# Attention's TensorE work of a batch in six stretches, not seven: windowed attention and a snake MLP in one kernel

## The chip, the cores and the metric

The kernel runs on one core of a Trainium2 chip. The metric is device microseconds (us) of one execution. The core's engines each work through their own list of instructions in order: PE (TensorE: matmuls, with its weight loads shown apart as PEld), ACT (ScalarE), DVE (VectorE), POOL (GpSimd) and SP (SyncE, which issues DMAs). They wait for each other by semaphores alone.

## What is computed

Eight batches of eight heads, 576 tokens of width 64: attention in a band of 32 tokens to each side, plus eight global tokens that see and are seen by all; then, on all 4608 tokens, two matmuls with the snake function between them.

```python
scores = q @ k.T / sqrt(64)                    # per batch and head, 576 x 576
mask = |i - j| <= 32  or  i is global  or  j is global
attn = softmax(where(mask, scores, -1e9))
x = (attn @ v) as 4608 x 512
h = x @ w_in                                   # 512 -> 2048
g = h + sin(alpha * h)**2 / alpha
out = g @ w_out                                # 2048 -> 512
```

## The kernel before

The work alternates between two kinds of phase. `gemm1(b)` multiplies batch b's attention output `xT` by `w_in`, in 16 groups of 8 matmuls (line 1113); ACT takes the sine of a group (line 1160), DVE or ACT squares it, and DVE adds the linear part (line 1166, `H<-s,recipT,z`), which is the last reading of the group's PSUM bank. Group nt writes the banks `zn`, `zr`, `zd` in turn, so that the last, nt = 15, stands in `zn`, and nt = 14 in `zd`.

Then `phase_a(b + 1, b)` does the attention of batch b+1, and beside it runs `gemm2(b)`, the product with `w_out` (line 1218, banks `zo`), as filler: it is a generator, and each `fill(n)` in the attention's code issues its next n matmuls (128x512). When 16 of them have ended, ACT copies the block out (line 1225) and SP stores it.

Attention goes over four pairs of heads, hp 0 to 3. For one pair there are two units of scores, `scores(hp, 0)` and `scores(hp, 1)`, each of 14 small 64x64 matmuls (line 814), an exponential on ACT that reads their bank (line 822), and a multiplication with the mask on DVE (`cover`, line 831). `denominators(hp)` are 28 small matmuls of E with ones into `zd` (line 862), a logarithm on ACT (line 772), and a small sum of the same bank on DVE, `GD` (line 756). `inverse(hp)` is an exponential of that logarithm on ACT, `R` (line 779). `numerators(hp)` are 28 small matmuls of E with the values into `zn` (line 862 too), the product with R on DVE (`normalise`, line 908, `xT<-zn,R`), and a small sum `GN`. A unit that writes a bank waits until the last reader of the bank's earlier content is done. Scores go to the bank `zs` (the profile's `ring`) but for two of the eight units.

In short letters, s for scores, d for denominators, n for numerators, and the filler matmuls in parentheses, PE's list in one attention phase is: (7), s00 s01 (10), s10 s11 d0 (8), s20 n0 (5), s21 d1 (5), s30 n1 (5), s31 d2 (7), n2 d3 n3 (3). A run of units between two fillers is called a stretch here. There are seven stretches, and 50 filler matmuls around them (in the first such phase the 10 and the 8 are 9 and 9). `beside(hp)` adds DVE work of other kinds after some stretches: squares of the batch before (lines 1027 to 1031), and the placing of the next batch's queries (line 366). `place_globals` is a copy on ACT (lines 374, 377).

Batch 0 has an order of its own (`first_batch`), so the order described runs seven times, for batches 1 to 7. Pools: `pairp` holds E, four buffers; `logp` holds the logarithms, five.

Of the kernel before, what the change touches and what calls it, by code (L numbers as in the profile page):

```python
# [12 lines left out]
DT = mybir.dt  # L13
# [3 lines left out]
P = 128  # L17
# [3 lines left out]
WCOL = 120  # L21
# [228 lines left out]
def kernel(  # L250
# [11 lines left out]
    nc = tc.nc  # L262
    B, H, S, D = q.shape
# [4 lines left out]
    NT6 = NT12 // 2  # L268
    NK = KT + NG
    NHP = H // 2  # L270
# [20 lines left out]
    pairp = mctx.enter_context(tc.tile_pool(name="pairp", bufs=4))  # L291
# [79 lines left out]
    def place_globals(b, part, copy):  # L371

        if part == 0:
            copy(out=KX[b % 2][:, :, :, KT:NK], in_=kTg[:, :, None, :, b].to_broadcast([P, NHP, NT12, NG]))
        else:
            y = part - 1
            copy(
                out=globals_of(b, slice(0, P), y),
                in_=qTg[:, :, None, y::2, b].to_broadcast([P, NHP, 7, 4]),
            )  # L380

    def globals_of(b, rows, y):

        q0 = QX[b % 2][rows, :, y, PAD : PAD + 4]
        return bass.AP(
            tensor=q0.tensor, offset=q0.offset, ap=[list(q0.ap[0]), [2 * QROW, NHP], [SEG, 7], [1, 4]]
        )
# [74 lines left out]
    zn, zd = [banks.tile([P, 2, 512], DT.float32, name=name) for name in ("zn", "zd")]  # L462
# [286 lines left out]
    def begin(i):  # L749

        m = i // 2
        return SEG * m - PAD if i % 2 == 0 else SEG * m + 12

    def global_sums(b, hp, key, z):
        g0 = z[:, 0, 0, 0:4]
        nc.vector.tensor_reduce(
            out=(GN, GD)[key][:, hp, :, b].rearrange("p (c x) -> p x c", x=2),
            in_=bass.AP(
                tensor=g0.tensor, offset=g0.offset,
                ap=[list(g0.ap[0]), [256, 2], [1, 4], [512, 2], [SEG, 4]],  # L760
            ),
            axis=AX.XY, op=ALU.add,
        )

    def tokens(z):
        return z.rearrange("p k x c -> p (k x) c")[:, :, 0 : 3 * SEG].rearrange(
            "p k (m c) -> p k m c", c=SEG
        )[:, :, :, 4:]

    def logarithm(b, hp, den):  # L770
        L = logp.tile([P, 4, 3, KT], DT.float32, name="L")
        nc.scalar.activation(out=L[:], in_=den, func=AF.Ln, scale=2.0**-SHIFT)  # L772
        r0 = b * H + 2 * hp
        nc.sync.dma_start(out=LC[r0 : r0 + 2, :], in_=L[0:P:D].rearrange("p k m c -> p (k m c)"))
        return L

    def inverted(L):
        R = normp.tile([P, 4, 3, KT], DT.float32, name="R")
        nc.scalar.activation(out=R[:], in_=L[:], func=AF.Exp, scale=-1.0, bias=shift[:, 0:1])
        return R  # L780

    def attention(b, beside):
# [7 lines left out]
        Es, Ls, Rs, begun = {}, {}, {}, set()  # L790
        ring = tc.alloc_tile_pool(name="ringp", bufs=1, space=PSUM)
        zs = ring.tile([P, 2, 512], DT.float32, name="ring")
# [3 lines left out]
        def windows(half):  # L796


            last = half * (NT6 - 1)
            return [(half * NT6 + m, m, 16 * (m == 0 == half), 60 - 16 * (m == half * last > 0)) for m in range(NT6)] + [  # L800
                (NT6 - half, last, 44 * half, 16 + 44 * half)
            ]

        def scores(hp, g):
            z = {(0, 1): zd, (1, 1): zn}.get((hp, g), zs) if b else (zs, zn)[g]
            for e in range(NT6 + 1):
                for half in range(2):
                    i, m, c0, c1 = windows(half)[e]
                    if m // G3 != g:
                        continue  # L810
                    s0 = PAD + begin(i)
                    for t in range(2):
                        rows = slice(t * D, (t + 1) * D)
                        nc.tensor.matmul(  # L814
                            out=z[half * D : (half + 1) * D, t, 0 : G3 * WCOL].rearrange(
                                "p (m x c) -> p m x c", x=2, c=60
                            )[:, m % G3, :, c0:c1],
                            lhsT=kx[rows, hp, i, :],
                            rhs=qx[rows, hp, :, s0 + c0 : s0 + c1],
                            start=True, stop=True, skip_group_check=True,  # L820
                        )
            nc.scalar.activation(out=weights(hp, g), in_=z[:, :, 0 : G3 * WCOL], func=AF.Exp, scale=scale)  # L822
            if b:
                cover(hp, g)

        def weights(hp, g):
            return Es[hp][:, :, G3 * g : G3 * (g + 1), :].rearrange("p t m c -> p t (m c)")

        def cover(hp, g):
            Eg = weights(hp, g)  # L830
            nc.vector.tensor_tensor(  # L831
                out=Eg, in0=Eg,
                in1=MASKT[:, None, G3 * g : G3 * (g + 1), :].rearrange("p o m c -> p o (m c)").to_broadcast(
                    [P, 2, G3 * WCOL]
                ),
                op=ALU.mult,
            )

        def nd(hp, key):


            if b == 0:
                t = zd if key or hp == last else (pair["zr"], zn)[hp % 2]
            else:
                t = (zn, zd)[key] if hp < last else (pair["zr"] if key else zd)
            return t[:].rearrange("p k (x c) -> p k x c", x=2)

        def products(hp, key):


            for e in range(NT6 + 1):
                for half in range(2):
                    i, m, c0, c1 = windows(half)[e]
                    s0 = begin(i)
                    lo, hi = (0, CUT + 4) if half == 0 else (CUT, QLEN)
                    if e == NT6:
                        lo, hi = (lo, CUT) if half == 0 else (CUT + 4, hi)
                    a, z = max(s0 + c0, lo), min(s0 + c1, hi)
                    rows = slice(half * D, half * D + NK)
                    for t in range(2):  # L860
                        bank = (hp, key, half, t)
                        nc.tensor.matmul(  # L862
                            out=nd(hp, key)[t * D : (t + 1) * D, half, :, a - half * CUT : z - half * CUT],
                            lhsT=ones[rows, 0:D] if key else values(b, rows, half, i, 2 * hp + t),
                            rhs=Es[hp][rows, t, m, :].rearrange("p (x c) -> p x c", x=2)[:, :, a - s0 : z - s0],
                            start=bank not in begun, stop=True, skip_group_check=True,
                        )
                        begun.add(bank)
# [21 lines left out]
        def denominators(hp):  # L890
            products(hp, 1)
            Ls[hp] = logarithm(b, hp, tokens(nd(hp, 1)))
            global_sums(b, hp, 1, nd(hp, 1))

        def inverse(hp):
            Rs[hp] = inverted(Ls[hp])
# [6 lines left out]
        def numerators(hp):  # L903
            products(hp, 0)
            normalise(hp)

        def normalise(hp):
            nc.vector.tensor_tensor(
                out=xT[:, hp, 0:S].rearrange("p (k m c) -> p k m c", k=4, c=KT), in0=tokens(nd(hp, 0)),
                in1=Rs[hp][:], op=ALU.mult,  # L910
            )
            global_sums(b, hp, 0, nd(hp, 0))
# [49 lines left out]
        last = NHP - 1  # L962
# [2 lines left out]
            return  # L965
        fill(START)
        beside(-1)
        for hp in range(NHP):
            newest[0] = Es[hp] = pairp.tile([P, 2, NT6, WCOL], DT.bfloat16, name="E")
            scores(hp, 0)  # L970
            if hp > 1:
                inverse(hp - 2)
                numerators(hp - 2)
                fill(FIRST[hp])
            scores(hp, 1)
            if hp and 0 < b and b + 1 < B:
                place_globals(b + 1, hp - 1, nc.scalar.copy)
            if hp:
                denominators(hp - 1)
            fill((SECOND_FIRST if b == 1 else SECOND)[hp])  # L980
            beside(hp)
        release_ring()
        inverse(last - 1)
        numerators(last - 1)
        denominators(last)
        products(last, 0)
        inverse(last)
# [288 lines left out]
    waiting, copied, at_group, newest = [], [None], [None], [None]  # L1276

    def fill(n):
        while n and waiting:
            if next(waiting[0], None) is None:  # L1280
                waiting.pop(0)
            else:
                n -= 1

    START = 7
    FIRST, SECOND, SECOND_FIRST = (0, 0, 5, 5), (10, 8, 5, 7), (9, 9, 5, 7)
    AFTER_COPY = 2

    NEAR = 3
# [70 lines left out]
    E = mybir.EngineType  # L1360
# [34 lines left out]
```

## Time and profile before

| | |
|---|---|
| time, median of 3 runs | 340.67 us (340.37 to 340.89) |
| the profiled execution's own time | 340.73 us |
| span of its profile | 339.0 us |
| busy: PE, ACT, DVE, POOL | 310.8, 278.5, 253.9, 142.5 us |
| filler matmuls `zo` (line 1218) | 134.3 us busy |
| granted TensorE clock | 9 tenths or more in all 40 slices |

A busy PE is not PE at its peak: the ends of matmuls are modelled, and the small matmuls of attention overlap each other. The chain of waits tells how much time each piece adds to the path: its rows give the start, the time to the next piece of the path, and the piece. An attention phase spans about 15 us on PE, one of `gemm1` about 20 us.

### The profile page before, as it was taken

How to read it: one execution, taken by the hardware profiler on the slowest of the kernel's cores; microseconds unless marked ns; L12 is line 12 of the kernel's file. 1: busy time of each engine (PE TensorE's matmuls, PEld its weight loads, DVE VectorE, ACT ScalarE, POOL GpSimd, SP SyncE). 2: the span in 40 equal slices, each digit the busy share in tenths (PEclk: the TensorE clock that was granted, in tenths of full speed). 3: DMA queues.
4: the chain of work that ended last, by engine and by line, in shares of the span. 5: the costliest groups of instructions: out<-in, count | busy, mean ns of one | idle time of the engine just before them, and what ended most of it. 6: DMA issues, size and time to landing. Idle time of an engine off the chain costs nothing.

```text
span 339.0 us, 11821 instructions
## 1 busy us (share of the span) xinstructions
PE 310.8 (92%) x4753; PEld 202.9 (60%) x4812; DVE 253.9 (75%) x485; ACT 278.5 (82%) x405; POOL 142.5 (42%) x296
## 2 busy tenths in 40 slices
PE   0778999999999999999999999999999999999994
PEld 0665765567556765667556755676566755665543
DVE  4784896877885888687886788578858788778930
ACT  6784888988999889988898889888888888889621
POOL 7983323339615761656345652458060000003600
PEclk9999999999999999999999999999999999999999
DMA  7999999989999999999959993799999311010232
GB/s 105 114 167 205 187 223 162 169 135 129 191 144 112 197 121 131 105 122 186 151 87 138 170 168 81 78 116 201 164 115 140 68 33 69 1 33 0 80 93 68
DMA packets 141941, 42.00 MB, mean 124 GB/s; under 512 B 126426, under 2 KB 136794, under 8 KB 141882
## 3 DMA queue, kind: packets, MB, share of 16 engines
q0 software_dynamic: 100096, 18.51, 69.6%
q1 hardware_dynamic: 41786, 22.69, 34.9%
q8 instruction: 38, 0.62, 0.8%
q14 instruction: 21, 0.17, 0.2%
HBM read 41.95 MB, written 20.77 MB: 185 GB/s over the span
## 4 chain that ended last, share of the span: by engine, by line
PE 77%; DVE 7%; ACT 6%; issue 4%; DMA 3%; POOL 2%; DVEq 0%; POOLq 0%; ACTq 0%
PE zo L1218 32%; PE zn L1113 13%; PE zr L1113 10%; PE zd L1113 9%; PE ring L814 4%; DVE H L1166 3%; PE zd L862 3%; ACT sb L1160 2%; PE zn L862 2%; DVE s L1165 1%; DMA H<-in_q_dram 1%; DMA out_dram<-osb 1%; ACT L988 1%; ACT s L1163 1%; ACT L L772 1%
## 5 line engine op out<-in xcount | busy, mean ns | idle before, releaser
L1218 PE MATMUL zo<-w_out,H 128*128 128x512 bf16 (+1 forms) x517 | 134.3, 377 | 6.1 <-issue 5.1
L1113 PEld LDWEIGHTS <-w_in 128*128 128x128 bf16 x1024 | 100.3, 98 | 46.0 <-issue 10.0
L1218 PEld LDWEIGHTS <-H 128*128 128x128 bf16 x592 | 53.6, 98 | 46.2 <-issue 0.4
L1113 PE MATMUL zn<-xT,w_in 128*128 128x288 bf16 (+1 forms) x384 | 58.0, 291 | 3.5 <-DVE H L1166 2.8
L1113 PE MATMUL zr<-xT,w_in 128*128 128x288 bf16 x320 | 48.5, 291 | 0.3
L1160 ACT ACTIVATE sb<-zn,alphaT 128x576 bf16<-128x576 f32 (+1 forms) x48 | 35.6, 742 | 14.7 <-PE zn L1113 14.2
L1166 DVE SCALAR_TENSOR_TENSOR H<-s,recipT,zn 128x576 bf16<-128x576 bf16 (+1 forms) x48 | 39.5, 822 | 10.4 <-ACT s L1163 6.5
L1113 PE MATMUL zd<-xT,w_in 128*128 128x288 bf16 x320 | 46.3, 288 | 0.4 <-DVE H L1166 0.2
L1165 DVE TENSOR_TENSOR s<-sb 128x576 bf16<-128x576 bf16 (+1 forms) x70 | 32.6, 465 | 14.4 <-ACT sb L1160 14.2
L822 ACT ACTIVATE E<-ring 128x720 bf16<-128x720 f32 x46 | 35.9, 780 | 8.7 <-PE ring L814 8.2
L1163 ACT ACTIVATE s<-sb 128x576 bf16<-128x576 bf16 (+1 forms) x58 | 40.0, 689 | 1.8
L831 DVE TENSOR_TENSOR E<-E,MASKT 128x720 bf16<-128x720 bf16 x64 | 33.4, 529 | 8.0 <-ACT E L822 6.1
L1166 DVE SCALAR_TENSOR_TENSOR H<-s,recipT,zd 128x576 bf16<-128x576 bf16 (+1 forms) x40 | 32.9, 822 | 7.6 <-ACT s L1163 5.0
L1166 DVE SCALAR_TENSOR_TENSOR H<-s,recipT,zr 128x576 bf16<-128x576 bf16 (+1 forms) x40 | 32.9, 822 | 6.5 <-ACT s L1163 4.9
L344 POOL DMA_DIRECT2D kd<-in_k_dram x48 | 31.2, 653 | 9.1 <-issue 7.3
L1160 ACT ACTIVATE sb<-zd,alphaT 128x576 bf16<-128x576 f32 (+1 forms) x40 | 29.6, 739 | 5.2 <-PE zd L1113 5.1
L1160 ACT ACTIVATE sb<-zr,alphaT 128x576 bf16<-128x576 f32 (+1 forms) x40 | 29.6, 740 | 4.3 <-PE zr L1113 4.3
L1208 POOL COPY H<-H 128x11 bf16 (+1 forms) x16 | 7.2, 452 | 57.6 <-DVE H L1166 56.7
L346 POOL DMA_DIRECT2D vd<-in_v_dram x48 | 30.4, 643 | 1.8 <-issue 1.3
L1225 ACT COPY osb<-zo 128x512 f32<-128x512 f32 (+1 forms) x36 | 21.0, 582 | 10.7 <-PE zo L1218 7.0
L346 POOL DMA_DIRECT2D qd<-in_q_dram x40 | 25.3, 633 | 8.2 <-issue 5.1
L814 PEld LDWEIGHTS <-KX 64*64 64x64 bf16 x896 | 15.5, 113 | 19.7 <-issue 18.8
(170 smaller groups left out, 375.3 us busy)
## 6 DMA issues: line engine op xcount, KB each, us to landing
VF<-vd SPq DMA_DIRECT2D x14, 336.0 KB
kd<-in_k_dram POOLq DMA_DIRECT2D x48, 72.0 KB, 4.6
vd<-in_v_dram POOLq DMA_DIRECT2D x48, 72.0 KB, 3.8
qd<-in_q_dram POOLq DMA_DIRECT2D x40, 72.0 KB, 6.3
w_out<-in_moe_w_out_dram POOLq DMA_DIRECT2D x2, 1024.0 KB, 26.0
out_dram<-osb SPq DMA_DIRECT2D x7, 256.0 KB
out_dram<-osb SPq DMA_DIRECT2D x8, 224.0 KB
out_dram<-osb SPq DMA_DIRECT2D x8, 192.0 KB
```

The lines of the kernel that those rows point to most:

```text
L344: nc.gpsimd.dma_start(out=dst[:, :, h], in_=src.rearrange("(i a) d -> a i d", a=KT))
L346: nc.gpsimd.dma_start(out=dst[:, h], in_=src)
L814: nc.tensor.matmul(out=z[half * D : (half + 1) * D, t, 0 : G3 * WCOL].rearrange("p (m x c) -> p m x c", x=2, c=60)[:, m % G3, :, c0:c1], l ...
L822: nc.scalar.activation(out=weights(hp, g), in_=z[:, :, 0 : G3 * WCOL], func=AF.Exp, scale=scale)
L831: nc.vector.tensor_tensor(out=Eg, in0=Eg, in1=MASKT[:, None, G3 * g : G3 * (g + 1), :].rearrange("p o m c -> p o (m c)").to_broadcast([P, ...
L1113: nc.tensor.matmul(out=h_part, lhsT=w_in[:, c, nt * P : (nt + 1) * P], rhs=xT[:, c, lo:hi], start=(c == 0), stop=(c == CT - 1), skip_group ...
L1160: nc.scalar.activation(out=sb[:, 0:W], in_=h, func=AF.Sin, scale=alphaT[:, nt : nt + 1])
L1163: nc.scalar.activation(out=s2[:, 0:W], in_=sb[:, 0:W], func=AF.Square)
L1165: nc.vector.tensor_tensor(out=s2[:, 0:W], in0=sb[:, 0:W], in1=sb[:, 0:W], op=ALU.mult)
L1166: nc.vector.scalar_tensor_tensor(out=H2[:, nt, r0 : r0 + W], in0=s2[:, 0:W], scalar=recipT[:, nt : nt + 1], in1=h, op0=ALU.mult, op1=ALU.add,)
L1218: nc.tensor.matmul(out=ops[:, cols], lhsT=H2[:, nt, blk * P : (blk + 1) * P], rhs=w_out[:, nt, cols], start=(nt == 0), stop=(nt == NT - 1) ...
L1225: nc.scalar.copy(out=osb[:, cols], in_=ops[:, cols])
```

## The change

The loop over pairs becomes a table `STEPS` that says which units a stretch holds and how many filler matmuls follow it. In the short letters the new list is: (7), s00 s01 s10 (13), s11 d0 s20 (8), s21 d1 n0 (7), s30 d2 n1 (7), s31 n2 (5), d3 n3 (3). These are six stretches; the units and the 50 filler matmuls are the same. The two units whose bank changes are s10, which moves from `zs` to `zn`, and s20, which moves from `zs` to `zn`; s11 moves from `zn` to `zs`. `inverse(step - 2)` stands at the start of a step, and `place_globals` at its end, behind the units.

```diff
         def scores(hp, g):
-            z = {(0, 1): zd, (1, 1): zn}.get((hp, g), zs) if b else (zs, zn)[g]
+            z = {(0, 1): zd, (1, 0): zn, (2, 0): zn}.get((hp, g), zs) if b else (zs, zn)[g]
...
-        for hp in range(NHP):
-            newest[0] = Es[hp] = pairp.tile([P, 2, NT6, WCOL], DT.bfloat16, name="E")
-            scores(hp, 0)
-            if hp > 1:
-                inverse(hp - 2)
-                numerators(hp - 2)
-                fill(FIRST[hp])
-            scores(hp, 1)
-            if hp and 0 < b and b + 1 < B:
-                place_globals(b + 1, hp - 1, nc.scalar.copy)
-            if hp:
-                denominators(hp - 1)
-            fill((SECOND_FIRST if b == 1 else SECOND)[hp])
-            beside(hp)
+
+        def score(hp, g):
+            if g == 0:
+                newest[0] = Es[hp] = pairp.tile([P, 2, NT6, WCOL], DT.bfloat16, name="E")
+            scores(hp, g)
+
+        for step, (blocks, n) in enumerate(STEPS):
+            if step > 1:
+                inverse(step - 2)
+            for what, *args in blocks:
+                {"s": score, "d": denominators, "n": numerators}[what](*args)
+            if 0 < step < NHP and b + 1 < B:
+                place_globals(b + 1, step - 1, nc.scalar.copy)
+            fill(n)
+            if step < NHP:
+                beside(step)
         release_ring()
-        inverse(last - 1)
-        numerators(last - 1)
         denominators(last)
...
-    FIRST, SECOND, SECOND_FIRST = (0, 0, 5, 5), (10, 8, 5, 7), (9, 9, 5, 7)
+    STEPS = (
+        ((("s", 0, 0), ("s", 0, 1), ("s", 1, 0)), 13),
...
+        ((("s", 3, 1), ("n", 2)), 5),
+    )
```

PE, the end of s01 in the attention of batch 3, before:

```order
L814 MATMUL zd<-QX_96,KX_94 64x2x16
L1218 LDWEIGHTS H_97
L1218 MATMUL zo_125<-w_out,H_97 128x512
L1218 LDWEIGHTS H_97
L1218 MATMUL zo_125<-w_out,H_97 128x512
```

And now, with what a matmul waits for in brackets:

```order
L814 MATMUL zd<-QX_96,KX_94 64x2x16
L814 LDWEIGHTS KX_94
L814 MATMUL zn<-QX_96,KX_94 64x2x44 [waits DVE_49]
L814 LDWEIGHTS KX_94
L814 MATMUL zn<-QX_96,KX_94 64x2x44
```

Between s01 and the first filler matmuls now stand 14 matmuls of s10, whose first waits for DVE, whose list holds the last group's `H<-s,recipT,zn` as the reader of `zn`.

ACT, the attention of batch 3 from its first exponential to the first R (the exponentials are s00, s01 and so on in the order of the short letters), before:

```order
L822 ACTIVATE E<-ring 128x2x360
L822 ACTIVATE E<-zd 128x2x360
L1225 COPY osb<-zo_125 128x512
L822 ACTIVATE E<-ring 128x2x360
L822 ACTIVATE E<-zn 128x2x360
L374 COPY KX_93<-kTg 128x4x12x8
L772 ACTIVATE L<-zd 128x576
L822 ACTIVATE E<-ring 128x2x360
L779 ACTIVATE R<-L,shift 128x576
L1225 COPY osb<-zo_126 128x512
L822 ACTIVATE E<-ring 128x2x360
L377 COPY QX_95<-qTg 128x4x7x4
```

And now:

```order
L822 ACTIVATE E<-zn 128x2x360
L1225 COPY osb<-zo_125 128x512
L822 ACTIVATE E<-ring 128x2x360
L772 ACTIVATE L<-zd 128x576
L822 ACTIVATE E<-zn 128x2x360
L374 COPY KX_93<-kTg 128x4x12x8
L1225 COPY osb<-zo_126 128x512
L779 ACTIVATE R<-L,shift 128x576
L822 ACTIVATE E<-ring 128x2x360
L772 ACTIVATE L<-zd 128x576
L377 COPY QX_95<-qTg 128x4x7x4
```

The exponentials of s00 and s01 stand ahead of these rows as before. The logarithm of d0 and the exponential of s20 now stand ahead of the copy KX, and the copy out of `zo_126` ahead of the first R.

DVE in the same phase, from the last of the squares to the second `GN`, before:

```order
L1031 TENSOR_TENSOR RM<-RM,SQ 128x576
L831 TENSOR_TENSOR E<-E,MASKT 128x2x360
L908 TENSOR_TENSOR xT<-zn,R 128x576
L756 TENSOR_REDUCE GN<-zn 128x2x4
L831 TENSOR_TENSOR E<-E,MASKT 128x2x360
L756 TENSOR_REDUCE GD<-zd 128x2x4
L366 COPY QX_95<-qt 128x4x6x48 x2
```

And now:

```order
L1031 TENSOR_TENSOR RM<-RM,SQ 128x576
L831 TENSOR_TENSOR E<-E,MASKT 128x2x360
L756 TENSOR_REDUCE GD<-zd 128x2x4
L908 TENSOR_TENSOR xT<-zn,R 128x576
L756 TENSOR_REDUCE GN<-zn 128x2x4
L366 COPY QX_95<-qt 128x4x6x48 x2
```

The sum `GD` of d1 moved from behind the first `xT<-zn,R` to ahead of it.

3 rows, old and new, of the table STEPS are left out of this document.

## The prediction

> **What bounds the kernel now.** I read the page first, for the busy engines and the shares of the path.
>
> ```profile
> PE 310.8 (92%) x4753; PEld 202.9 (60%) x4812; DVE 253.9 (75%) x485; ACT 278.5 (82%) x405; POOL 142.5 (42%) x296
> PE 77%; DVE 7%; ACT 6%; issue 4%; DMA 3%; POOL 2%; DVEq 0%; POOLq 0%; ACTq 0%
> ```
>
> PE carries 77% of the path. Then I read the chain of waits in one attention phase, that of batch 3 (columns: start, time to the next piece of the path, piece; x is the number of instructions recorded).
>
> ```profile
> 126.87 0.28 PE ring L814 x12
> 127.14 0.16 PE zd L814 x12
> 127.31 0.17 issue
> 127.48 2.10 PE zo L1218 x9
> 129.58 0.28 PE ring L814 x12
> 129.86 0.16 PE zn L814 x12
> 130.02 0.32 PE zd L862 x22
> 130.34 0.16 issue
> 130.50 1.67 PE zo L1218 x7
> 132.93 1.03 PE zo L1218 x4
> ```
>
> All of it is PE: in this phase PE waits for no other engine. The first unit of a stretch costs 0.28 us, a second unit of scores 0.16, a unit of denominators or numerators behind another unit 0.32, and "issue" of 0.16 to 0.17 stands between the units and the filler. The filler runs are of 10, 8 and 5 matmuls, so one more costs (2.10 - 1.67) / 2 = 0.215, and a run is about 0.05 shorter than its number times that.
>
> **The change, part by part.**
>
> *One stretch less.* The units and the filler are the same in number, so what goes is the cost of beginning and ending a stretch: 0.28 - 0.16 = 0.12 for the first unit, plus 0.17, less the 0.05 of the run, 0.24 us in a phase. Seven phases give -1.7 us. The Trainium skill's page TensorEngine Tiling (Array Packing), section Key Properties, says that a change of tiling mode drains TensorE; by that rule a stretch less saves one drain on each side, which agrees with the 0.28 against 0.16 here, and by it alone the sum would be this saving.
>
> *s10 in the bank `zn`.* It stands third in the first stretch, and `zn` still holds group 15 of `gemm1`, which DVE's line 1166 reads last. So s10 starts no sooner than that reader's end. These are, for batches 1 to 7, the end of s01 (start plus time) and the reader of `zn`; the row of batch 3's s01 is above. The row after them is the time from such a reader to PE's next matmul.
>
> ```profile
> 53.80 0.17 PE zd L814 x12
> 53.16 0.81 DVE L1166 SCALAR_TENSOR_TENSOR H<-s,recipT,zn 128x576 bf16<-128x576 bf16 x1
> 90.30 0.17 PE zd L814 x12
> 90.42 0.81 DVE L1166 SCALAR_TENSOR_TENSOR H<-s,recipT,zn 128x576 bf16<-128x576 bf16 x1
> 126.73 0.81 DVE L1166 SCALAR_TENSOR_TENSOR H<-s,recipT,zn 128x576 bf16<-128x576 bf16 x1
> 163.54 0.16 PE zd L814 x12
> 163.42 0.81 DVE L1166 SCALAR_TENSOR_TENSOR H<-s,recipT,zn 128x576 bf16<-128x576 bf16 x1
> 199.90 0.17 PE zd L814 x12
> 199.81 0.81 DVE L1166 SCALAR_TENSOR_TENSOR H<-s,recipT,zn 128x576 bf16<-128x576 bf16 x1
> 236.78 0.17 PE zd L814 x12
> 236.29 0.81 DVE L1166 SCALAR_TENSOR_TENSOR H<-s,recipT,zn 128x576 bf16<-128x576 bf16 x1
> 273.63 0.17 PE zd L814 x12
> 273.51 0.81 DVE L1166 SCALAR_TENSOR_TENSOR H<-s,recipT,zn 128x576 bf16<-128x576 bf16 x1
> 109.31 0.04 issue
> ```
>
> Reader's end plus 0.04 less s01's end: 0.04, 0.80, 0.28, 0.57, 0.59, 0.19 and 0.56 us, 3.03 in all. The 13 filler matmuls are queued behind s10 on PE, so nothing fills the gap: +3.0 us. Before, s10 went to `zs` and stood behind 10 filler matmuls, where no such wait could show.
>
> *ACT and DVE in the middle of the phase.* Before, ACT met each unit of scores in small portions. Now it gets three exponentials early, stands idle during the long filler run of 13, and then has a full list. These rows of batch 3 (the timeline: start, duration, instruction) give what it takes from one ACT start to the next when ACT is the limit, and DVE's steps.
>
> ```profile
> 127.45 0.77 ACT L822 ACTIVATE E<-ring 128x720 bf16<-128x720 f32 x1
> 128.11 0.77 ACT L822 ACTIVATE E<-zd 128x720 bf16<-128x720 f32 x1
> 129.92 0.77 ACT L822 ACTIVATE E<-ring 128x720 bf16<-128x720 f32 x1 [0.57 <-PE ring L814]
> 131.24 0.88 ACT L374 COPY KX<-kTg 128x384 bf16<-128x384 bf16 x1
> 132.00 0.67 ACT L772 ACTIVATE L<-zd 128x576 f32<-128x576 f32 x1
> 133.19 0.81 ACT L779 ACTIVATE R<-L,shift 128x576 f32<-128x576 f32 x1
> 133.86 0.61 ACT L1225 COPY osb<-zo 128x512 f32<-128x512 f32 x1
> 134.32 0.82 ACT L822 ACTIVATE E<-ring 128x720 bf16<-128x720 f32 x1
> 138.86 0.65 ACT L772 ACTIVATE L<-zd 128x576 f32<-128x576 f32 x1
> 139.40 0.59 ACT L1225 COPY osb<-zo 128x512 f32<-128x512 f32 x1
> 132.71 0.23 DVE L756 TENSOR_REDUCE GD<-zd 128x8 f32<-128x64 f32 x1 [0.79 <-ACT L L772]
> 132.85 0.75 DVE L1029 TENSOR_TENSOR SQ<-SQ 128x1152 bf16<-128x1152 bf16 x1
> 134.94 0.75 DVE L908 TENSOR_TENSOR xT<-zn,R 128x576 bf16<-128x576 f32 x1
> 135.61 0.22 DVE L756 TENSOR_REDUCE GN<-zn 128x8 f32<-128x64 f32 x1
> ```
>
> From start to start: exponential 0.66, KX 0.76, R 0.67, copy of a block 0.46, logarithm 0.54; an exponential starts 0.06 behind its scores (129.58 + 0.28 to 129.92); on DVE, `GD` 0.14, `xT` 0.67. `GD` starts 0.04 behind the logarithm's end (132.67 to 132.71), though both only read the bank. I now walk through batch 3 with the new order.
>
> PE: s10 runs from 127.58 to 127.74, then 0.17 and 13 filler matmuls (2.10 + 3 x 0.215 = 2.74) to 130.65. The second stretch, s11, d0, s20, ends its units at 130.93, 131.25 and 131.41, and with 0.17 and 8 filler matmuls (1.67) the third begins at 133.25: s21 to 133.53, d1 to 133.85, n0 to 134.17, 0.17, 7 filler matmuls (1.03 + 2 x 0.215 = 1.46). The fourth begins at 135.80, s30 ends at 136.08, and PE would then want d2.
>
> ACT from s11's exponential on: 130.99, d0's logarithm 131.65, s20's exponential 132.19, KX 132.85, the block's copy 133.61, R 134.07, s21's exponential 134.74, d1's logarithm 135.40 to 136.07. d2 writes `zd`, which d1's `GD` must have read: 136.11 to 136.34, so d2 starts at 136.38, a wait of 0.30. `xT` of pair 0 stands behind that `GD` on DVE: 136.25, its `GN` 136.92 to 137.14. n1 writes `zn` and can start at 137.18; PE wants it at 136.38 + 0.32 = 136.70: a wait of 0.48. Together 0.78 us in this phase. If the block's copy does not fall into this piece of ACT's list, all moves 0.46 earlier, d2 does not wait, and n1 waits 0.3; but the same chain repeats a step later for n2 (it needs the `GN` of pair 1) and for d3 (it needs s31's exponential, behind an R, and its mask). I take 0.78 for each of the seven phases, +5.5 us. Bounds: none at all if ACT's list is shorter by 0.8 us than walked, and 1.6 in a phase (twice the walked wait, n2 or d3 as late as d2 and n1), so 0 to 11 us; the walk of this phase is the nearest row. The Trainium skill's page PSUM — Partial Sum Buffer, section PSUM bank collisions raise a hardware error, says that two engines must not touch one bank and quadrant at once, two reads included; the row of `GD` behind the logarithm agrees. If the two could read together, `GD` and all behind it would come about 0.7 us sooner and the 5.5 would nearly go.
>
> *Restart.* A unit behind a wait costs 0.28, as the first of a stretch, not 0.16: between 0 and 0.12 for each wait. The waits in the middle are set by ACT and DVE and swallow most of it; I count one of 0.12 in a phase, +0.8 us, with 0 and 2.5 (three in each) as ends.
>
> *Edits that cost nothing here.* s20 in `zn` needs s10's exponential, which by the walk starts at 128.77, long before 131.25. `place_globals` is read one batch later. POOL's casts of batch 2 wait for a newer E, under its idle time (42% busy). SP's stores of logarithms move past stores of blocks; they have five buffers. The last stretch loses n2, so d3's logarithm comes 0.32 earlier in it, but PE's lateness of over 1 us is more than that.
>
> Sum: 340.73 - 1.7 + 3.0 + 5.5 + 0.8 = 348.3 us for the profiled execution, whose time is 0.06 above the median: 348.3 against 340.67, 2.2% slower.
>
> **The rivals.** *Only the first wait.* ACT keeps up in the middle (its busy share is 82%, and PE waits for nothing in the phase quoted). Then 340.7 - 1.7 + 3.0 = 342.0. Against it: the walk has ACT without a gap from 130.99 to 136.07.
>
> *Faster.* Mechanism: the time of beginning and ending a stretch is all that counts, since the wait of s10 is covered: the reader of `zn` is finished sooner, or the time lost is given back where PE waits for the sine at the head of `gemm1`. Price 1.7 us, 339.0. It decides if the first waits together stay below 1.7 us (3.0 by the rows) and the middle ones vanish. The page on tiling named above speaks for this one. Against it: seven pairs of rows, six of them with a wait of 0.19 or more.
>
> *Worse than forecast.* Each phase's late `GN` and `cover` hold up n2 and d3 as well, 1.2 us or more in the middle: 340.7 - 1.7 + 3.0 + 8.4 + 0.8 = 351. The walk's fourth stretch ends late, which gives ACT time to catch up; that speaks against.
>
> *The change does not do what it says*, and nothing moves: excluded by the order of PE's list, which has 14 more matmuls ahead of the first filler.
>
> **How the numbers follow.** Forecast (both kinds of wait, 345 to 350.5): 0.66. Only the first wait (341.5 to 345): 0.17. Faster (339): 0.05. Worse than 350.5: 0.10. The rest, 0.02, is no change. A measurement of this kernel can tell about 0.2% (0.7 us) from no change. So faster 0.05, same 0.02, slower 0.93. The range takes in the forecast and the rival of the first wait, 341.9 to 350.5, which leaves 0.17 out.
>
> **What would show it.** In the chain of waits of the changed kernel, six stretches in a phase; between s01 and s10 of batches 2 to 7 a gap on PE put down to DVE line 1166 (0.2 to 0.8 us); in the fourth stretch PE waits ahead of d2 or n1 for `GD` or `GN`, line 756; ACT without idle time from s11's exponential to d1's logarithm. The phase from s00 to the first matmul of `gemm1` is longer by 0.6 to 1.4 us. If PE shows no waits inside the third and fourth stretches, the middle term is wrong; if s10 starts right behind s01, the first term is.

## The result and the profile after

The changed kernel takes 350.02 us (median of 6 runs, 349.14 to 350.77); the kernel before, run beside it, takes 340.78 (6 runs, 339.87 to 342.27). The ratio is 1.0277, 95% interval 1.0255 to 1.0298: 9.2 us slower. The profiled execution took 349.14 us with a span of 347.4, which is 8.4 more than the 340.73 and 339.0 of the one before.

The page of the changed kernel, its first and its fourth part (busy time, and the shares of the path that ended last):

```profile
PE 319.0 (92%) x4812; PEld 204.4 (59%) x4812; DVE 254.7 (73%) x485; ACT 277.5 (80%) x405; POOL 142.5 (41%) x296
PE 52%; DVE 15%; ACT 15%; DMA 10%; issue 4%; POOL 2%; SPq 1%; DVEq 0%; ACTq 0%; POOLq 0%
```

Busy times of ACT, DVE and POOL are what they were. The path is not: PE carried 77% of it and now 52%, while DVE went from 7 to 15%, ACT from 6 to 15% and DMA from 3 to 10%. The DMA's part has to be read with care. Eight of its points are one transfer, that of `w_out`, which the chain follows back from one filler matmul in batch 1: the transfer takes 29.26 us of the chain, but PE waits only 0.30 us for it. (A share of PE's busy time shows nothing of all this: it was 92% and is 92%.)

PE's waits for DVE in attention, of the whole run (columns: waiting piece, what it waited for, us in total, times, the longest). The changed kernel:

```profile
PE zn L814 <- DVE H L1166: 3.1, 6, 0.8
PE zn L862 <- DVE GN L756: 3.1, 10, 0.6
PE zd L862 <- DVE GD L756: 1.2, 4, 0.5
```

The kernel before has only the last of these, once:

```profile
PE zd L862 <- DVE GD L756: 0.7, 1, 0.7
```

That one stands in batch 0, whose order did not change, and one of the four of the changed kernel (0.5) stands there too. So 3.1 + 3.1 + 0.7, about 7 us of waits, 19 in number, are new, and each is at a bank: s10 for the last reader of `gemm1`'s group 15, numerators for `GN`, denominators for `GD`.

This is the chain of waits of batch 3 in the changed kernel (start, time to the next piece of the path, piece), from s10 to d3:

```profile
129.66 0.82 DVE H L1166
130.48 0.04 issue
130.53 0.35 PE zn L814 x11
130.87 2.92 PE zo L1218 x13
133.79 0.33 PE ring L814 x12
...
134.14 0.53 ACT E L822
...
134.81 0.65 ACT L L772
135.45 0.66 ACT E L822
136.11 0.68 ACT KX L374
136.79 0.43 issue
137.23 0.81 ACT R L779
138.03 0.67 ACT E L822
138.70 0.02 issue
138.73 0.53 DVE E L831
139.26 0.01 issue
139.27 0.23 DVE GD L756
139.49 0.66 DVE xT L908
140.16 0.14 DVE GN L756
140.30 0.04 issue
140.34 0.50 PE zn L862 x25
140.84 1.62 PE zo L1218 x7
```

The rows of batch 3 before were all PE. Now the path leaves PE twice. It starts in DVE's line 1166, ahead of s10. And from the scores of s11 on it runs through ACT's list without a gap to speak of (exponential, logarithm, exponential, KX, the block's copy behind the row of 0.43, R, exponential), then through DVE (`cover`, `GD`, `xT`, `GN`), and comes back to PE at n1. The rows 0.35 and 0.50 are the third thing to see: s10 and n1 behind their waits cost 0.35 and 0.50, where the rows before had 0.16 for a second unit of scores and 0.32 for numerators behind another unit. One row also corrects a reading: the run of 13 fillers shows all 13 and no row of "issue" ahead of it, where the run of 10 before showed 9 behind an "issue" of 0.17. That 0.17 was no pause of PE but the first filler matmul, whose record is missing: the profile before has 517 of the 576 matmuls of line 1218, this one has all.

The phases, from the first matmul of s00 to the first matmul of the next `gemm1`, read from the timelines, batches 1 to 7 (us):

| kernel | 1 | 2 | 3 | 4 | 5 | 6 | 7 | sum |
|---|---|---|---|---|---|---|---|---|
| before | 14.70 | 14.74 | 14.83 | 14.70 | 14.75 | 15.30 | 14.62 | 103.64 |
| changed | 16.91 | 16.42 | 15.86 | 16.17 | 16.15 | 15.74 | 16.13 | 113.38 |

The sum is 9.74 longer. The `gemm1` stretches between the phases differ by 0.08 at most. Batch 1's phase began 1.0 earlier (52.47 against 53.45), ahead of all that was changed; the rest of the difference to the span's 8.4 lies in those small amounts and behind the last phase.

### The profile page after: what moved, and what is told of

Read it like the earlier page. It is cut to its first block, busy times and chain, and to the rows that moved or that the text cites. A ratio compares the mean times of both kernels' runs of the same rounds, so it can differ in the third digit from the quotient of the medians.

```text
span 347.4 us, 11868 instructions
## 1 busy us (share of the span) xinstructions
PE 319.0 (92%) x4812; PEld 204.4 (59%) x4812; DVE 254.7 (73%) x485; ACT 277.5 (80%) x405; POOL 142.5 (41%) x296
## 4 chain that ended last, share of the span: by engine, by line
PE 52%; DVE 15%; ACT 15%; DMA 10%; issue 4%; POOL 2%; SPq 1%; DVEq 0%; ACTq 0%; POOLq 0%
PE zo L1218 21%; PE zn L1113 10%; DMA w_out<-in_moe_w_out_dram 8%; PE zr L1113 8%; PE zd L1113 7%; DVE H L1166 5%; ACT E L822 4%; ACT sb L1160 3%; DVE xT L908 2%; ACT L L772 2%; DVE E L831 2%; DVE s L1165 2%; DMA gidx<-in_global_idx_dram 2%; ACT osb L1225 1%; ACT s L1163 1%
## 5 line engine op out<-in xcount | busy, mean ns | idle before, releaser
L1218 PE MATMUL zo<-w_out,H 128*128 128x512 bf16 (+1 forms) x576 | 146.1, 377 | 0.5 <-DMA w_out<-in_moe_w_out_dram 0.3
L831 DVE TENSOR_TENSOR E<-E,MASKT 128x720 bf16<-128x720 bf16 x64 | 33.7, 531 | 23.2 <-ACT E L822 21.3
L822 ACT ACTIVATE E<-ring 128x720 bf16<-128x720 f32 x39 | 30.4, 779 | 10.4 <-PE ring L814 10.0
L814 PEld LDWEIGHTS <-KX 64*64 64x64 bf16 x896 | 16.2, 112 | 20.5 <-issue 19.7
```

The costliest lines, as they stand in the source:

```text
L814: nc.tensor.matmul(out=z[half * D : (half + 1) * D, t, 0 : G3 * WCOL].rearrange("p (m x c) -> p m x c", x=2, c=60)[:, m % G3, :, c0:c1], l ...
L831: nc.vector.tensor_tensor(out=Eg, in0=Eg, in1=MASKT[:, None, G3 * g : G3 * (g + 1), :].rearrange("p o m c -> p o (m c)").to_broadcast([P, ...
L1218: nc.tensor.matmul(out=ops[:, cols], lhsT=H2[:, nt, blk * P : (blk + 1) * P], rhs=w_out[:, nt, cols], start=(nt == 0), stop=(nt == NT - 1) ...
```

## The experiments

Eleven kernels were run. The first five take the forecast's terms apart one by one. The others look for the remaining time and for a faster six-stretch version. "Before" means the kernel before, run on the same chip beside each group; its medians were 340.56, 340.25 and 340.54. Differences between two kernels are those of their medians; the ratio, which goes by pairs of runs on one chip, can differ from them by up to 0.8 us.

### Four filler matmuls moved ahead of s00

Four of the 13 filler matmuls go ahead of s00, so that `gemm1`'s last reader has ended when PE comes to s10. The filler stays the same in number.

```diff
-    START = 7
+    START = 11
-        ((("s", 0, 0), ("s", 0, 1), ("s", 1, 0)), 13),
+        ((("s", 0, 0), ("s", 0, 1), ("s", 1, 0)), 9),
```

> The changed kernel with four filler matmuls moved from behind the first three units to ahead of them (11 and 9 in place of 7 and 13). Theory: the wait of s10 for group 15's last reader (3.1 us in six waits) goes, as 4 x 0.215 = 0.86 us is more than its longest, 0.81, and the waits in the middle stay: 350.0 - 3.1 - 0.7 for restarts = about 346. Rival: ACT's late list sets the phase whatever PE does at its start, so the first scores, coming later, push the middle back by as much as the wait was: 349 to 350.

Measured: 346.39 us, 1.0148 (1.0109 to 1.0188) of before, 3.6 less than the changed kernel. In PE's waits the row of line 1166 ahead of line 814 is gone, and those in the middle have stayed:

```profile
PE zn L862 <- DVE GN L756: 3.0, 10, 0.6
PE zd L862 <- DVE GD L756: 1.5, 4, 0.7
```

So the first wait is a term of its own, worth at least the 3.1 us of its row. What it costs beyond that can be read from the starts of s01 and s10 in batch 3 (the timeline), first in the changed kernel, then in this one:

```profile
129.91 0.33 PE L814 MATMUL zd<-QX,KX 64*64 64x120 bf16 x14
130.53 0.35 PE L814 MATMUL zn<-QX,KX 64*64 64x88 bf16 x14 [0.28 <-DVE H L1166]
130.29 0.33 PE L814 MATMUL zd<-QX,KX 64*64 64x120 bf16 x14
130.46 0.33 PE L814 MATMUL zn<-QX,KX 64*64 64x88 bf16 x14
```

Without a wait s10 begins 0.17 behind s01, while s01's last matmuls are still under way (they end 0.33 behind its start). With it s10 begins 0.62 behind s01: 0.45 later, of which the profile lists 0.28, since it counts from the (modelled) end of s01's last matmul. The other 0.17 is the overlap of the two units, lost. From the start of s00 to the first filler these three units take 0.62 us here in six of the seven phases, and in the changed kernel 1.62, 1.08, 1.38, 1.42, 1.02 and 1.38 in batches 2 to 7. Less 0.62 and less the listed wait (0.81, 0.28, 0.58, 0.61, 0.21, 0.57) that leaves 0.18 or 0.19 each time.

### s10 alone, in the kernel before

Here the kernel before keeps its seven stretches, and only s10 moves into the first of them and into the bank `zn`; s11 takes `zs` in its place.

```diff
-            z = {(0, 1): zd, (1, 1): zn}.get((hp, g), zs) if b else (zs, zn)[g]
+            z = {(0, 1): zd, (1, 0): zn}.get((hp, g), zs) if b else (zs, zn)[g]
...
-            newest[0] = Es[hp] = pairp.tile([P, 2, NT6, WCOL], DT.bfloat16, name="E")
-            scores(hp, 0)
+            if hp != 1:
+                newest[0] = Es[hp] = pairp.tile([P, 2, NT6, WCOL], DT.bfloat16, name="E")
+                scores(hp, 0)
...
+            if hp == 0:
+                newest[0] = Es[1] = pairp.tile([P, 2, NT6, WCOL], DT.bfloat16, name="E")
+                scores(1, 0)
```

> The kernel before with one unit moved: s10 into the first stretch, third, in the bank zn, and s11 into zs; seven stretches, all filler runs as before. Theory: the first wait alone, 3.1 us and a restart of 0.12 in six phases, 344 to 344.6; no saving, no waits of PE in the middle. Rival, the wait is covered by slack later in the phase: 340.8 to 341.5.

Measured: 344.06 us (10 runs), 1.0092 (1.0061 to 1.0123): 3.5 slower than before by the medians, 3.1 by the ratio, with this edit alone. The wait is the one of the changed kernel to the tenth (the line numbers move by four):

```profile
PE zn L814 <- DVE H L1170: 3.1, 6, 0.8
```

Done alone and undone alone, the first wait is worth much the same, 3.5 and 3.6 us by the medians, and 3.1 of it is the wait itself. The phases say what each costs beyond its length: those of batches 2, 3, 4, 5 and 7 are 3.56 us longer in sum (77.20 against 73.64; batch 6 is left out, since the profile of before has a gap of its own in it, and its phase there is 0.6 longer than its neighbours). Their five waits are 2.9 by the rows (3.1 less batch 6's 0.2), which leaves 0.13 each. That is too low, because four of these five phases of before hold small delays of their own (14.70 to 14.83, where its shortest, batch 7, has 14.62). From s00 to the first filler the units take here what they take in the changed kernel, in all six batches, so by them it is 0.18 to 0.19 again.

### The copies of global tokens on POOL

`place_globals`, the KX and QX copies, leaves ACT's list, which the walk had made the cause of the middle waits.

```diff
-                place_globals(b + 1, step - 1, nc.scalar.copy)
+                place_globals(b + 1, step - 1, nc.gpsimd.tensor_copy)
```

> The changed kernel with the three copies of place_globals in a phase on POOL in place of ACT, so that ACT's list between s20's exponential and the first R is 0.76 us shorter. Theory that ACT's list makes the middle waits: 2 to 5 us faster, 345 to 348, with the waits of PE for GD and GN fewer and the first waits (3.1 us) unchanged. Rival, DVE's squares make them: within 1 us of 350.

Measured: 347.74 us, 1.0189 (1.0147 to 1.023), 2.3 less than the changed kernel. The middle waits of batches 1 to 7 go from 3.8 to 1.6, the row of `GD` is gone, and the row of the first wait is the same to the tenth:

```profile
PE zn L862 <- DVE GN L756: 1.6, 7, 0.5
```

So ACT's list sets more than half of the middle waits by these copies alone. The profiled execution also holds waits of 0.7 and 2.5 us in batch 1 for the DMA of `w_out`, of which more below.

### DVE without its squares

The rival cause for the middle: the squares of the attention output and their sums, lines 1027 to 1031, of which 1029 to 1031 stand between `cover` and `GD` on DVE. They serve only to tell, at the kernel's end, whether the sine's argument could leave its range and another path has to be taken. This kernel leaves them out in the attention phases.

```diff
-            if 0 <= part < 2:
-                square_x(b_moe, part)
```

> The changed kernel without the squares of the batch before in the attention phases (they serve only a check of ranges, so the kernel leaves out that part of its check). They are 2.9 us of DVE in a phase, and stand on the path in the chain of waits in four of the seven phases. Theory that ACT's list makes the middle waits: the squares only stand where DVE would wait for ACT anyway, under 1 us, 349 to 350. Rival that DVE makes them: 1.5 us in each of four phases, 6 us, 344.

Measured: 349.87 us, 1.0263 (1.0224 to 1.0302), as slow as the changed kernel.

```profile
DVE E L831 <- ACT E L822: 39.8, 36, 2.4
PE zn L862 <- DVE GN L756: 3.0, 11, 0.4
```

DVE now stands idle for 39.8 us ahead of its masks, waiting for ACT's exponentials, where it was 21.3 in the changed kernel (and 6.1 before), and PE waits for `GN` as long as ever. DVE's squares are not the cause. They filled time in which DVE had to wait for ACT.

### What one more stretch costs

The kernel before, with the run of 8 filler matmuls behind s10 s11 d0 broken into 3 and 5: an eighth stretch, in the same order of units.

```diff
+            if hp == 1:
+                fill(3)
             if hp:
                 denominators(hp - 1)
-            fill((SECOND_FIRST if b == 1 else SECOND)[hp])
+            fill((SECOND_FIRST if b == 1 else SECOND)[hp] - 3 * (hp == 1))
```

> The kernel before with one stretch more: of the 8 filler matmuls behind s10, s11 and d0, three go ahead of d0, so that a phase has eight stretches and the same units and filler. Theory: a stretch costs 0.24 us where PE is the limit, 7 x 0.24 = 1.7 us, 342.3 against 340.6. Rival, beginning and ending a stretch is hidden or is less than the rows say: 340.6 to 341.2.

Measured: 342.09 us, 1.0048 (1.0032 to 1.0064) of 340.25. That is 1.6 us by the ratio (1.8 by the medians), 0.23 to 0.26 for each of seven, and the rows of batch 3 gave 0.24 (0.12 + 0.17 - 0.05). Its profiled execution, the slowest of the six, has two waits for `w_out` in batch 1, 4.1 us together, so the phases behind it are the better witness: those of batches 2, 3, 4, 5 and 7 are 1.18 longer in sum, 0.24 each. The Trainium skill's page TensorEngine Tiling (Array Packing), section Key Properties, says that a change of tiling mode drains TensorE; this run agrees, and some 0.24 us is what leaving the small tiles once more and coming back cost here.

### Filler moved to where PE waits

With the first wait covered as above, three filler matmuls more go from the first run to the third.

```diff
-    START = 7
+    START = 11
-        ((("s", 0, 0), ("s", 0, 1), ("s", 1, 0)), 13),
+        ((("s", 0, 0), ("s", 0, 1), ("s", 1, 0)), 6),
-        ((("s", 2, 1), ("d", 1), ("n", 0)), 7),
+        ((("s", 2, 1), ("d", 1), ("n", 0)), 10),
```

> The changed kernel with its 50 filler matmuls spread anew: 11 ahead, then 6, 8, 10, 7, 5, 3 (in place of 7, 13, 8, 7, 7, 5, 3). The first run is shorter, so ACT gets s11 earlier, and the third is longer, so d2 and n1 come later. Theory that both kinds of wait are a matter of where the filler lies: most of them go, 341 to 343. Rival, ACT has no room in a phase of six stretches and its lateness moves to n2 and d3: 345 to 347, no better than with 11 and 9.

Measured: 344.9 us (343.8 to 347.99), 1.0154 (1.0119 to 1.0188), between what the two theories expected. The waits for `GN` fall to 1.6 us, five of them, and the phases of batches 3 to 7 to between 13.92 and 14.31, where the kernel with four fillers ahead of s00 alone had 14.47 to 14.55. Either of two things can have done it: s11's exponential comes earlier, as the walk would have it, and three fillers more stand ahead of d2 and n1. The run does not tell them apart. It did not bring the time back to that of before.

### All covers together

Filler moved, numerators ahead of denominators in two stretches, and the copies on POOL.

```diff
-    START = 7
+    START = 11
-                place_globals(b + 1, step - 1, nc.scalar.copy)
+                place_globals(b + 1, step - 1, nc.gpsimd.tensor_copy)
-        ((("s", 0, 0), ("s", 0, 1), ("s", 1, 0)), 13),
+        ((("s", 0, 0), ("s", 0, 1), ("s", 1, 0)), 7),
-        ((("s", 2, 1), ("d", 1), ("n", 0)), 7),
-        ((("s", 3, 0), ("d", 2), ("n", 1)), 7),
+        ((("s", 2, 1), ("n", 0), ("d", 1)), 10),
+        ((("s", 3, 0), ("n", 1), ("d", 2)), 6),
```

> Six stretches with all that helped put together: filler 11, 7, 8, 10, 6, 5, 3, numerators ahead of denominators in the third and fourth stretch (so that xT does not stand behind GD on DVE), and place_globals on POOL. Theory: the waits are nearly gone, the stretch less is worth up to 1.7 us, but a restart and some waits for the last units remain: 340 to 342, no clear difference from the kernel before. Rival: with the waits gone the whole 1.7 us comes, 339.

Measured: 344.69 us, 1.013 (1.0106 to 1.0153). The expectation was missed by over 2 us. The phases of batches 2 to 7 are 13.86 to 14.44, and with the 0.86 of four more fillers that now run ahead of them 14.7 to 15.3, nearly down to those before; but batch 1's is 17.89. Its timeline shows why:

```profile
57.20 1.01 PE L1218 MATMUL zo<-w_out,H 128*128 128x512 bf16 x2 [2.10 <-DMA w_out<-in_moe_w_out_dram]
```

The second half of `w_out` is still under way when the 17th filler matmul, the first that reads it, comes. In the changed kernel this wait is there too, but short:

```profile
55.74 1.02 PE L1218 MATMUL zo<-w_out,H 128*128 128x512 bf16 x4 [0.30 <-DMA w_out<-in_moe_w_out_dram]
```

Before, the 17th stood behind d0 and began at 56.72, without a wait. That is 3.27 us after s00 began (53.45), and in the changed kernel it is 3.27 after s00 too (55.74 against 52.47), 0.30 of it the wait. So the new order, in which 20 fillers stand ahead of s11 where 16 stood ahead of d0, asks for `w_out` 0.30 sooner, and the other 1.0 is batch 1's phase, which began earlier in that execution. The old order waits as well when the phase begins early: 1.68 us in the kernel before with its copies in `gemm1` (s00 at 52.12), 2.77 in the one with the eighth stretch (51.62).

### The copies on POOL, in the kernel before

```diff
-                place_globals(b + 1, hp - 1, nc.scalar.copy)
+                place_globals(b + 1, hp - 1, nc.gpsimd.tensor_copy)
```

> The kernel before with place_globals on POOL in place of ACT, to set beside the same edit in the changed kernel, where it gave 2.3 us. Theory that PE, not ACT, is the limit of the seven-stretch phase: no difference, 340 to 341. Rival, ACT's list limits this kernel too: 1.5 us or more faster, 339 or less.

Measured: 342.24 us, 1.0051 (1.0033 to 1.0068): slower by 1.7 us by the ratio (2.0 by the medians), where no difference was expected, though ACT has less to do. A place of its timeline (start, duration, instruction):

```profile
91.03 2.13 DVE L831 TENSOR_TENSOR E<-E,MASKT 128x720 bf16<-128x720 bf16 x2 [0.17 <-ACT E L822]
91.26 0.87 POOL L374 COPY KX<-kTg 128x384 bf16<-128x384 bf16 x1
92.06 0.71 POOL L377 COPY QX<-qTg 128x112 bf16<-128x112 bf16 x1
```

And the same two masks in the kernel before:

```profile
91.40 1.19 DVE L831 TENSOR_TENSOR E<-E,MASKT 128x720 bf16<-128x720 bf16 x2 [0.16 <-ACT E L822]
```

DVE's work grows from 1.19 to 2.13 us while POOL copies beside it, and PE now has a wait of a new kind, that of d0 for the mask:

```profile
PE zd L862 <- DVE E L831: 1.0, 4, 0.3
```

The phases of batches 2 to 5, where these four waits stand, are 1.9 us longer in sum (60.92 against 59.02). So POOL is not free for these copies. In the changed kernel with the copies on POOL three masks of batch 2 take 2.53 us and not 1.86, so there too a part of what was gained on ACT was lost on DVE; and with all covers together the stretch s11 d0 s20 takes 1.25 to 1.37 us in batches 1 to 4, where the changed kernel has 0.78.

### The copies inside gemm1, on ACT

```diff
-            if 0 < step < NHP and b + 1 < B:
-                place_globals(b + 1, step - 1, nc.scalar.copy)
...
+            if 0 < b and b + 1 < B and nt in (5, 7, 9):
+                place_globals(b + 1, (nt - 5) // 2, nc.scalar.copy)
```

> The changed kernel with place_globals taken out of the attention phases and put, still on ACT, into gemm1's groups 5, 7 and 9 of the same batch. It shortens ACT's list in a phase by 0.76 + 2 x 0.28 = 1.3 us without giving POOL anything. Theory that ACT's list makes the middle waits: 3 to 5 us faster than the changed kernel, 345 to 347, first waits (3.1 us) as they were, fewer waits for GD and GN. Rival, the list has slack and only the distance between units counts: 349 to 350.

Measured: 349.05 us, 1.0247 (1.0224 to 1.0271), 1.0 less than the changed kernel. The time lies in the rival's range, but the rival's reason does not hold: the waits in the middle did fall, as on POOL (the row of the first wait is as it was):

```profile
PE zn L862 <- DVE GN L756: 1.8, 7, 0.6
```

The phases of batches 3 to 6 are shorter by about 0.5 each (15.31, 15.57, 15.82, 15.22). But five of the six `gemm1` with the copies in them are 0.34 to 0.39 longer: there the copies stand among the sines in ACT's list, which PE's next groups wait for. The chain of waits has the KX copy on it, with 0.76 to 0.79 us, in exactly these five; in batch 4's, which is only 0.01 longer, it has none. Batch 2's phase also has a gap of 0.94 us on PE that waits for nothing the profile shows.

### The copies inside gemm1, in the kernel before and with all other covers

First the kernel before with the copies in `gemm1`:

```diff
-            if hp and 0 < b and b + 1 < B:
-                place_globals(b + 1, hp - 1, nc.scalar.copy)
...
+            if 0 < b and b + 1 < B and nt in (5, 7, 9):
+                place_globals(b + 1, (nt - 5) // 2, nc.scalar.copy)
```

Second the kernel with all covers, its copies in `gemm1` and not on POOL (the diff is against that kernel):

```diff
-            if 0 < step < NHP and b + 1 < B:
-                place_globals(b + 1, step - 1, nc.gpsimd.tensor_copy)
...
+            if 0 < b and b + 1 < B and nt in (5, 7, 9):
+                place_globals(b + 1, (nt - 5) // 2, nc.scalar.copy)
```

> The kernel before with place_globals on ACT in gemm1's groups 5, 7 and 9. Theory that PE is the limit in its attention phases: no difference, 340 to 341. Rival, ACT's shorter list helps the phases whose end goes through ACT (three of seven in the chain of waits): up to 1 us faster, 339.5.

> As the last attempt with six stretches (filler 11, 7, 8, 10, 6, 5, 3, numerators ahead of denominators in the third and fourth stretch), but with place_globals on ACT in gemm1, not on POOL. Theory that POOL's copies slowed DVE's masks there (two masks took 2.13 us beside POOL's copy in the kernel before with that edit): 341 to 343, better than the 344.7 of that attempt. Rival, that attempt lost its time elsewhere: 344 to 345.

Measured: the kernel before with the copies moved takes 341.96 us (12 runs), 1.0043 (1.0019 to 1.0067), and the six-stretch one 346.13 (343.05 to 347.1), 1.0157 (1.0119 to 1.0195). The first is slower by 1.4 us where half of that at most was expected, the second missed by 3.

In the profiles of the two the phases of batches 3 to 6 agree: 14.62 to 14.64 with seven stretches, and with six 13.71 to 13.86, to which the 0.86 of four more fillers ahead comes, 14.57 to 14.72. PE's waits for `GN` in the latter are down to 0.4 us in all. Thus, with the listed waits nearly gone, six stretches were no shorter than seven. The starts show what is left: s30 n1 d2 takes 1.01 to 1.11 us in these four phases (the first filler behind it, whose record is missing, put 0.22 ahead of the second), and s31 n2 0.61 to 0.73, where the same units took 0.92 (the kernel with all covers) and 0.61 without a delay. In each of the four phases n1 begins 0.25 to 0.35 behind s30, and 0.19 with all covers. Such delays are too short to be listed as waits, but they come to 0.2 to 0.3 us in a phase, as much as a stretch less can bring.

The profile of the first also has a gap on PE in the middle of a unit of denominators in batch 2, and PE waits there for nothing that the profile shows (the chain of waits):

```profile
98.19 0.11 PE zd L862 x8
98.29 1.66 issue
99.95 0.41 PE zd L862 x17
```

A gap of 1.24 us stands in a unit of denominators of the same phase in the six-stretch one. These gaps, and waits for `w_out` in batch 1 of 1.7 and 0.4 us, are in these profiled executions; how much of them other executions have, a profile of one can't tell. The scatter of the kernels with four fillers more at the start (343 to 348 us) was not settled. None of the eleven is faster than the kernel before.

## Why the prediction was right, point by point

The forecast was 348.3 us, slower by 2.2%, and the time is 350.02, slower by 2.8%. The direction and both places of the waits came out as walked. Three terms had the wrong size, and that the sum came so near is in part luck: the middle, 1.7 us too high, made up for most of the restarts, 2.6 too low.

*A stretch less, -1.7.* Its price of 0.24 is right for a stretch more (the run with the eighth stretch). In the changed kernel only a part of it is gained. Its phases of batches 3 to 7, less their listed waits (0.84, 1.15, 1.12, 0.71, 1.10) and less 0.18 for each of three restarts, are 14.48 or 14.49 all five. Seven stretches without a delay take 14.62 (batch 7 before; 14.61 to 14.64 in the kernel before with its copies in `gemm1`). That is 0.14 in a phase, 1.0 us in seven. The 0.17 in the price was a matmul whose record is missing and not a pause, but the price does not change by it: the whole run of ten, 0.17 + 2.10, is 0.12 longer than ten times 0.215, and 0.12 is what the prediction took, 0.17 - 0.05.

*s10 in `zn`, +3.0.* Right. The seven pairs of rows gave 3.03; the profile has 3.1, in six waits (the seventh, of 0.04 by the rows, is too short to be listed). Moving s10 alone cost 3.1 to 3.5, and covering it gave 3.6 back, its restarts included. The rival in which the time is given back at the head of `gemm1` is refuted: the `gemm1` stretches are as long as before.

*The middle, +5.5.* The mechanism was right, the size too high: `GN` 3.1 and `GD` 0.7, 3.8 together. In batch 3 the walk had n1 begin 10.38 us after s00 began; it began at 140.34, 10.62 after 129.72. It had d2 wait 0.30 for `GD` and n1 0.48 for `GN`; these rows of the timeline show 0.26 and 0.30:

```profile
139.54 0.50 PE L862 MATMUL zd<-E,ones 56*64 56x88 bf16 x28 [0.26 <-DVE GD L756]
140.34 0.50 PE L862 MATMUL zn<-E,VF 56*64 56x88 bf16 x28 [0.30 <-DVE GN L756]
```

n1 waits less only because d2 held PE longer ahead of it, and PE was later. ACT's list itself came as walked: measured from s00, every start from s11's exponential to d1's `GD` is 0.22 to 0.24 later than in the walk, and the restart of s10, at the head of it, is most of that. Then came the step from one batch to seven: not every phase has both waits, thirteen in all and not fourteen, and they are shorter on average (3.8 / 13 = 0.29 and not 0.39). That ACT is the cause was shown from both sides, by the copies taken off it (the waits fell from 3.8 to 1.6 or 1.8) and by the squares taken off DVE (3.0 of waits for `GN` remained of 3.1). What the remaining 1.6 hang on was not taken away by an edit of its own.

*Restart, +0.8.* This is the term that was too small, and the step of the prediction that failed. I counted one restart of 0.12 in a phase, because ACT and DVE were to swallow the others. They swallow none: the unit behind a wait has lost its overlap with the unit ahead of it, whoever ended the wait. Start to start it is 0.17 to 0.19 at each of the 19 waits; for the middle ones this is what is left when s30 d2 n1 (0.92 without a wait, batch 2) and s31 n2 (0.61, batches 3 and 4) and the listed waits are taken off. 19 x 0.18 is 3.4 us, above my upper bound of 2.5. Both the count, one where there are nearly three in a phase, and the size, 0.12, were too low.

*What was not in the sum.* Batches 1 and 2 hold 1.7 us more than 14.48, waits and restarts. In batch 1 it is 0.7: the wait for `w_out` with its restart, and a restart of s10 behind a wait that is not listed. In batch 2 it is 0.9: a gap of 0.42 us in n0 that waits for nothing the profile shows, 0.21 behind it, and 0.31 more in s31 n2. And the phases before were not free of delays either: they hold 1.3 us more than seven times 14.62, 0.7 of it in batch 6. Batch 1 has most of its growth of 2.2 us in the middle, with three waits of 1.15 together. The chain of waits there runs through DVE:

```profile
63.28 0.67 DVE SQ L1029
...
64.93 0.45 DVE E L831
65.37 0.14 DVE GD L756
65.51 0.66 DVE xT L908
66.17 0.14 DVE GN L756
```

Squares stand on the path here; without them, though, this phase is only 0.5 shorter (16.44).

*The sum again, by what was measured:* -1.0 (the stretch) + 3.1 (s10) + 3.8 (the middle) + 3.4 (the restarts) + 1.7 (batches 1 and 2) - 1.3 (delays of before) = 9.7, against 9.74 in the phases. All of it is read from one profiled execution of each kernel; how much of the last two terms other executions have is open. The phases grew by 0.44 to 2.21 each, where I said 0.6 to 1.4; the 1.0 us by which batch 1 began earlier hid part of that from the whole time.

*The expected signs.* Six stretches, the gaps at s10 in batches 2 to 7, and ACT without idle time from s11's exponential to d1's logarithm are all in the profile (in batch 3 ACT has none from 134.14 to beyond 141). `GD` did not wait for the logarithm alone: the mask of s21 ended at 139.26, just ahead of it, so ACT's exponential held DVE as much as its logarithm did.

## What to carry to other kernels

Before a unit is moved to another bank, find the bank's last reader and the work that now hides it: two rows of the trace for each phase gave this term of 3 us to a tenth. Count each new wait of PE at its listed length plus the overlap that the waiting unit loses with the one ahead of it (0.18 us here, for units of 14 and of 28 small matmuls alike), and look what the filler that moves with it reads for the first time. And an engine that is busy for 80% of the span can still be the limit over 5 us, when its work comes in one batch; walk its list there, start to start, rather than read its share.

## What was not expected of the hardware

POOL's small copies make DVE's masks slower: two masks take 2.13 us and not 1.19 (rows above). The Trainium skill's page SBUF — State Buffer, section Who interferes with whom, says that POOL and DVE share a pair of ports, and that a DVE instruction with two inputs in SBUF contends with a POOL instruction that reads SBUF. The rows of the masks, which have two inputs, agree with it. In the same kernel a DVE copy of 1 x 8 numbers (line 1182, batch 3) takes 1.58 us and not 0.15 and ends with POOL's KX copy, but it began 0.6 us ahead of that copy; what held it until then, the rows don't show.

PE stood for up to 1.66 us in the middle of one unit's matmuls, in the attention of batch 2, and waited for nothing that the profile shows. Six of the thirteen profiles have such a gap there, always in the stretch that begins with s21 (0.42 in the changed kernel, and 0.72, 0.94, 0.95, 1.24 and 1.66), and the kernel before has none there. What holds it there stays open.
